# Three buffers for the pairs of transposed p, its load a step later, and later stages shifted by a step

## The chip, the cores and the metric

The kernel runs on one core of a Trainium2 chip. The metric is device time in microseconds, the median of the runs made. Five engines work side by side, each on its own queue in program order: TensorE (PE in the profile, with its weight loads as PEld), VectorE (DVE), ScalarE (ACT), GpSimd (POOL), and SyncE (SP), which here only issues DMAs. A DMA whose semaphore is not there yet holds up every later DMA in SP's queue.

## What is computed

```python
xn = _layernorm(x)
# A: attention of all 2048 rows with the last W = 512 keys, 32 heads of 128
q = (xn @ wq).reshape(B, Sq, Hq, Dh)
p = softmax(einsum("bhqd,bhkd->bhqk", q, k) * Dh ** -0.5)
s = einsum("bhqk,bhkd->bhqd", p, v).reshape(B, Sq, Hq * Dh) @ wo
# B: gated MLP with a mix over the sequence
z = gelu(xn @ w_in); z1, z2 = z[..., :Fh], layernorm(z[..., Fh:])
g = w_sp @ z2 + b_sp
out = x + s * silu((z1 * g) @ w_out)
```

x is 2048 x 512, all in float32. Every matmul is made of three in float32r: each operand is split into a rounded part h and a rest l, and h h, h l and l h are summed (`mm3`, lines 63 to 67). So nearly every operand passes through a cast on ACT (the h) and a subtraction on POOL or DVE (the l, `rest`, line 59).

## The kernel before, in words

There are three stages: a short start (layernorm and transposes of the first eight row tiles), the attention loop, and the MLP's second half. The change is in the attention loop, which fills about three quarters of the time.

The loop of line 679 runs over steps t. Attention is cut into blocks: a block is one head and 512 rows of x, four steps of 128 rows each, and `where` (line 366) says which head and rows block b has. There are 128 blocks and so 512 steps (NSTEP). The first 64 blocks use the first 1024 rows, the rest the second 1024. Two blocks, eight steps, share one head's weights. Block b has steps 4b to 4b + 3. Each step is a software pipeline: the stages that run in step t belong to different earlier or later steps, by fixed distances (line 34). In program order, step t holds:

- loads of weights for later steps (lines 680 to 684, SP)
- `shares` of step t - ML (line 500): the cast of a quarter of pL to pT_h on ACT, and the rest pT_l on POOL
- `todo`: splits of weights that have arrived (ACT, POOL), and in steps 30 to some 217 the pieces of `later_x`
- `score` of step t (line 467): three matmuls to a PSUM bank of ps_step; the negated maximum nm of a row on DVE (line 474); the Exp on ACT, to prob (line 476)
- two or three matmuls of the q products of later blocks (line 447; 42 in 16 steps), each sum to a bank of ps_acc
- `pv` of step t - PL (line 509), three matmuls with pT; after a block's fourth, `pv_out` makes oT (ACT, and two rests on DVE)
- `outp` of step t - OL (line 525), three matmuls to a bank of ps_step, and the addition to sacc on DVE (line 535)
- `turned` of block t // 4 - 1, when t % 4 is 2 (line 494)
- `turn` of step t - 1 (line 478)
- the rests of `late`, on DVE; then `ends`, more DMAs

p must be transposed before `pv`. This is done in two halves. `turn` transposes 32 x 32 squares of prob on DVE into pB (line 485). A pB holds two steps, a pair; after the second one, SP stores it to DRAM as half of p_dram (line 490, in the steps t with t % 4 equal to 0 and 2). When both halves of block b are in DRAM, `turned` loads them into pL with the rows regrouped (line 498, four DMAs of 32 partitions each). So the path of p is Exp, transpose, store, load, cast and rest, `pv`. pB has two buffers (the default of pool ap, line 87), pL two, p_dram three, pT_h and pT_l four each. ps_step has four banks, from which every step takes one for its score and one for its `outp`.

`later_x` (line 265) prepares the second 1024 rows in four passes, p = 0 to 3, while the loop runs. A pass loads two row tiles a and b, normalizes and transposes them, and makes eight tiles of parts (`new_part`, line 302: b's two halves, a's two, then the sums T2, T1, T3, T4), each of which is stored to DRAM (x_dram). All these tiles come from pool xq (name rawx), five buffers of 2 KB a partition; a and b stay alive until the sums are made. A pass has 18 places, 13/5 of a step apart (line 603). At one place the stores of its list are issued ahead of its function: the stores of a's two parts stand in the same step as the cast of T2.

The last pieces of w_in are also loaded into xq in the loop's last steps, each eight steps before its split (line 564). The q products are evicted through tiles qs (line 453, three buffers). `ln_stats` (line 169) makes the mean and 1/sqrt(var + eps) of a pair of tiles; rs_t holds var + eps between the two POOL operations (line 72), and `row_stats` of `later_x` makes nb, minus mean times r.

Of the kernel before, what the change touches and what calls it, by code (L numbers as in the profile page):

```python
# [8 lines left out]
F32 = mybir.dt.float32  # L9
# [8 lines left out]
P = 128  # L18
# [10 lines left out]
NBLK = H * NQ  # L29
NSTEP = NBLK * 4  # L30
SCALE = DH ** -0.5


XL, QL, ML, PL, OL = 11, 7, 10, 12, 17
T8 = NT // 2
LEAD = 13
Q = 32
# [3 lines left out]
def mixer_kernel(ctx: ExitStack, tc: tile.TileContext, x, wh, w_in, w_sp, b_sp, w_out, out):  # L41
# [30 lines left out]
    def rsqrt(var, y, n, v):  # L72

        nc.gpsimd.tensor_scalar(v[:, :n], var, EPS, None, op0=OP.add)
        nc.gpsimd.tensor_tensor(y[:, :n], v[:, :n], power[:, :n], op=OP.pow)

    stats = ctx.enter_context(tc.tile_pool(name="stats", bufs=2))
# [7 lines left out]
    att = ExitStack()  # L85
# [1 line left out]
    ap = att.enter_context(tc.tile_pool(name="ap", bufs=2))  # L87
    wq = att.enter_context(tc.tile_pool(name="wq", bufs=2))
    zs = att.enter_context(tc.tile_pool(name="zs", bufs=2))
    xq = att.enter_context(tc.tile_pool(name="xq", bufs=5))  # L90
    sacc = sp.tile([P, T8, D], F32, name="sacc")


# [52 lines left out]


    GROUPS = [(a, a + 1) for a in range(4)] + [(a, a + 2) for a in range(4, T8, 2)]
    mv, rx = {}, {}
    X = {0: {}, 1: {}}  # L150

    def block():
# [16 lines left out]
    def ln_stats(tiles, key):  # L169
        mv[key] = stats.tile([P, 2, 2], F32, name="mv", bufs=5)  # L170
        for k, t in enumerate(tiles):
            stt = stats.tile([P, 6], F32, name="stt", bufs=4)
            nc.vector.bn_stats(stt, t)
            nc.vector.bn_aggr(mv[key][:, k, :], stt)
        n = len(tiles)
        r = stats.tile([P, 2], F32, name="rs_r", bufs=5)
        rsqrt(mv[key][:, :n, 1], r, n, stats.tile([P, 2], F32, name="rs_t", bufs=4))
        for k in range(n):
            rx[key + k] = mv[key][:, k, 0:1], r[:, k:k + 1]

# [84 lines left out]
    def later_x(p):  # L265

        a, b = T8 + p, T8 + 4 + p
        t, nb = {}, {}

        def load():  # L270
            for i in (a, b):
                t[i] = xq.tile([P, 512], F32, name="rawx")
                nc.sync.dma_start(t[i], x[i * P:(i + 1) * P, :])

        def row_stats():
            ln_stats([t[a], t[b]], 100 * (p + 1))
            for k, i in enumerate((a, b)):
                mean, r = rx[100 * (p + 1) + k]
                nb[i] = stats.tile([P, 1], F32, name="nb", bufs=2)
                nc.gpsimd.tensor_scalar(nb[i], mean, r, -1.0, op0=OP.mult, op1=OP.mult)  # L280

        def apply(i):
            nc.scalar.activation(t[i], t[i], AF.Identity, bias=nb[i], scale=rx[100 * (p + 1) + (i == b)][1])

        def parts(i, n):
            ps = flip(t[i]).rearrange("p c q -> p (c q)")
            if n:
                nc.scalar.copy(t[i][:, :256], ps[:, :256])
            for h in range(2):
                sl = ps[:, 256 * h:256 * h + 256]  # L290
                hi, lo = new_part((h, n))
                nc.scalar.copy(hi, sl)
                late.append((rest, nc.vector, lo, sl, hi))
            if n:
                late.append((rest_f32, t[i][:, 256:], ps[:, 256:], t[i][:, :256]))
            else:
                late.append((row_sums, ps, t[b], t[a]))

        def rest_f32(to, x0, x1):
            nc.vector.tensor_tensor(to, x0, x1, op=OP.subtract)  # L300

        def new_part(k):
            st = t[k] = xq.tile([P, 512], F32R, name="rawx")
            return st[:, :256], st[:, 256:]

        def sum_part(k, src):
            hi, lo = new_part(k)
            nc.scalar.copy(hi, src())
            rest(nc.gpsimd, lo, src(), hi)

        def store(*ks):
            for k in ks:
                nc.sync.dma_start(xd[1, k][:, :, :, p * P:(p + 1) * P],
                                  t[k].bitcast(F32).rearrange("p (a c q) -> p a c q", a=2, q=P))

        def half(i, h):
            return lambda: t[i][:, 256 * h:256 * h + 256]

        seq = [load, None, None, None, None, row_stats, None,
               lambda: apply(b),  # L320
               lambda: parts(b, 1),
               lambda: apply(a),
               None,
               lambda: parts(a, 0),
               None,
               lambda: sum_part("T2", half(a, 1)),
               lambda: sum_part("T1", half(a, 0)),
               lambda: sum_part("T3", half(b, 1)),
               lambda: sum_part("T4", half(b, 0))]
        stores = {10: ((0, 1), (1, 1)), 13: ((0, 0), (1, 0)), 14: ("T2",), 15: ("T1",), 16: ("T3",), 17: ("T4",)}  # L330
        return [(f, stores.get(n, ())) for n, f in enumerate(seq + [None])], store
# [31 lines left out]
    pB = [None]  # L363
# [86 lines left out]
    def q_evict(g, k):  # L450
        ps = qps[g, BANK[k]]
        if k in (0, 2, 3):
            t = qps[g, "t", k] = ap.tile([P, 512], F32, name="qs", bufs=3)
            nc.scalar.activation(t, ps, AF.Copy, scale=SCALE)  # L454
        elif k in (1, 5):
            nc.vector.scalar_tensor_tensor(ps, ps, SCALE, qps[g, "t", {1: 0, 5: 2}[k]], op0=OP.mult, op1=OP.add)
        elif k == 4:
            t = qps[g, "t", 3]
            nc.vector.scalar_tensor_tensor(t, ps, SCALE, t, op0=OP.mult, op1=OP.add)
# [18 lines left out]
    def turn(t):  # L478

        b, j = divmod(t, 4)
        if j % 2 == 0:
            pB[0] = ap.tile([P, 4, 2, P], F32, name="pB")
        nc.vector.transpose(pB[0][:, :, j % 2, :].rearrange("p a (c q) -> p a c q", q=Q),  # L485
                            prob.pop(t).rearrange("p (a c q) -> p a c q", a=4, q=Q))
        if j == 0:
            pD[b] = dram.tile([2, P, 1024], F32, name="p_dram", bufs=3)
        if j % 2:
            nc.sync.dma_start(pD[b][j // 2], pB[0].rearrange("p a j f -> p (a j f)"))  # L490
        if j == 3:
            nc.vector.reciprocal(sums[b], sums[b])

    def turned(b):
        pL[b] = ap.tile([P, 8, 256], F32, name="pL")
        of = pD.pop(b).rearrange("s (i r) (a f) -> a r (s i) f", i=4, a=4)
        for a in range(4):
            nc.sync.dma_start(pL[b][Q * a:Q * a + Q], of[a])
# [50 lines left out]
    def plan(key, k, t, lead=6):  # L549
        loads.setdefault(max(T0, t - lead), []).append((key, k))  # L550
        at(t, lambda: split_piece(key, k, nc.vector if t >= NSTEP - 4 and k % 2 else nc.gpsimd))
# [9 lines left out]
    for n, ds in enumerate(((-16, -14, -12, -10), (-6, -4, -2, 2), (1, 4, 8, None), (13, None, 9, 11))):  # L561
        for k, d in enumerate(ds):
            if d is not None:
                plan(("w", n), k, NSTEP + d, 8)

    for key, k, d in ((("w", 2), 3, 7), (("w", 3), 1, 10)):
        loads.setdefault(NSTEP + d, []).append((key, k))
# [111 lines left out]
    for t in range(T0, T1):  # L679
        for key in loads.get(t, ()):  # L680
            if isinstance(key, int):
                load_q(key)
            else:
                load_piece(*key)
        bq, cq = divmod(t + QL, 4)
        bm, cm = divmod(t - ML, 4)
        bp, cp = divmod(t - PL, 4)
        bo, jo = divmod(t - OL, 4)
        i = t + XL
        if i < T8:  # L690
            ln_flip(i)
        if 0 <= bm < NBLK:
            shares(bm, cm)
        for f, args in todo.get(t, ()):
            f(*args)
        if 0 <= t < NSTEP:
            score(t)
        if i + 2 < T8:
            ln_apply(rows[i + 2], i + 2)
        if t in FILL:  # L700
            z1_piece(*FILL[t])
        if 0 <= bq < 4:
            qproj(bq, cq)
        g, s = divmod(t + LEAD, 16)
        if 0 < g < NG:
            q_products(g, s)
        if 0 <= bp < NBLK:
            pv(bp, cp)
        if 0 <= bo < NBLK:
            outp(bo, jo)  # L710
        if t in DRAIN:
            ps = z1_product(*DRAIN[t])
        if 0 <= bq < 4:
            qproj_out(bq, cq)
        for f, *args in q_events.get(t, ()):
            f(*args)
        if 0 <= bp < NBLK:
            pv_out(bp, cp)
        if t in DRAIN:
            z1_out(*DRAIN[t], ps)  # L720
        if t % 4 == 2 and 0 <= t // 4 - 1 < NBLK:
            turned(t // 4 - 1)
        if 0 <= t - 1 < NSTEP:
            turn(t - 1)
        while late:
            f, *args = late.pop(0)
            f(*args)
        for f, *args in ends.get(t, ()):
            f(*args)
# [279 lines left out]
```

## Time and profile before

| | us |
|---|---|
| median of 3 runs | 1965.47 |
| lowest and highest | 1961.61 and 1967.25 |
| the profiled execution | 1965.79 |
| its span, first to last instruction | 1964.0 |
| DVE idle ahead of line 485, until a store of p_dram had landed | 228.4 |
| PE idle ahead of the score's first matmul, until DVE's sacc | 81.2 |

The span is one execution; what lies around it is 1.8 us. "Busy" counts the time in which an engine has an instruction under way. In the lines of groups, the numbers after the bar are the busy time in us, the mean ns of one, then the idle time of the engine just before them and what ended it. In the windows the columns are the start and end, the length, the busy us of each engine with its instructions, the granted clock as a share, the mean share of time that the 16 DMA engines are busy, and GB/s. The lines themselves stand in the prediction.

### The profile page before, as it was taken

Reading aid. Unit: us, or ns where it says so; the run is one execution under the profiler, and the core shown is the slowest. Engines: PE = TensorE matmul, PEld = TensorE weight load, DVE = VectorE, ACT = ScalarE, POOL = GpSimd, SP = SyncE. Lnnn points to the kernel's source line nnn. Section 1 sums busy time; section 2 is a strip of 40 time slices with the busy share of each in tenths; the row PEclk is TensorE's granted clock in tenths of the full one; section 3 lists DMA queues with packets and bytes.
Section 4 is the critical chain, followed back from the end, with each engine's and each line's share of the span. In section 5 each row is a group of like instructions: output and inputs, shape, how many; then the busy total and the mean of one; then the engine's idle time right before and its main releaser. Section 6 shows DMA issues by size and latency. Waiting matters only on the chain.

```text
span 1964.0 us, 28248 instructions
## 1 busy us (share of the span) xinstructions
PE 1851.8 (94%) x8658; PEld 1551.2 (79%) x8658; DVE 1394.3 (71%) x2497; ACT 1187.8 (60%) x2631; POOL 1250.5 (64%) x1185
## 2 busy tenths in 40 slices
PE   8998999999999998899999999999999999999999
PEld 7776777777777776777777777777777899999998
DVE  5577888878888877778788778878887656333433
ACT  4666666767767666666667666666676535333422
POOL 3677788778888877777878778877887435000000
PEclk9999999999999999999999999999999999999999
DMA  5698898988998989898888988888889843544432
GB/s 174 197 267 215 229 268 232 245 246 236 252 252 236 252 236 327 227 256 232 243 216 225 242 227 229 238 226 223 226 241 252 240 145 115 188 145 160 155 128 93
DMA packets 277624, 429.16 MB, mean 219 GB/s; under 512 B 22272, under 2 KB 183808, under 8 KB 276320
## 3 DMA queue, kind: packets, MB, share of 16 engines
q1 hardware_dynamic: 272864, 421.72, 76.9%
q10 hardware_dynamic: 4608, 5.64, 0.8%
q8 instruction: 68, 1.11, 0.2%
q14 instruction: 84, 0.69, 0.1%
HBM read 260.55 MB, written 166.72 MB: 218 GB/s over the span
## 4 chain that ended last, share of the span: by engine, by line
DMA 37%; PE 34%; DVE 16%; ACT 6%; issue 4%; SPq 2%; POOL 1%; ACTq 0%; DVEq 0%; POOLq 0%
DMA p_dram<-pB 32%; DVE nm L474 5%; PE ps_g L67 4%; PE ps_g L66 4%; PE ps_g L65 4%; DVE pB L485 4%; DVE sacc L535 3%; DMA pL<-p_dram 3%; PE ps L65 3%; PE ps_a L65 3%; PE ps_a L66 3%; PE ps_a L447 3%; PE ps_a L67 2%; PE ps L67 2%; PE ps L66 2%
## 5 line engine op out<-in xcount | busy, mean ns | idle before, releaser
L59 POOL TENSOR_TENSOR pT_l<-pL,pT_h 128x512 fp32r<-128x512 f32 x507 | 655.5, 1293 | 313.0 <-ACT pT_h L505 284.9
L476 ACT ACTIVATE prob<-ps,nm 128x512 f32<-128x512 f32 x512 | 352.8, 689 | 384.3 <-DVE nm L474 381.1
L485 DVE STREAM_TRANSPOSE pB<-prob 128x512 f32<-128x512 f32 x512 | 359.1, 701 | 253.6 <-DMA p_dram<-pB 228.4
L447 PE MATMUL ps_a<-x,x 128*128 128x512 f32 x1302 | 381.4, 394 | 0.8 <-ACT qs L454 0.8
L535 DVE SCALAR_TENSOR_TENSOR sacc<-ps,sums,sacc 128x512 f32<-128x512 f32 x496 | 364.8, 736 | 20.6 <-PE ps L67 20.1
L505 ACT CAST pT_h<-pL 128x512 fp32r<-128x512 f32 x512 | 317.4, 620 | 97.8 <-DMA pL<-p_dram 70.2
L474 DVE TENSOR_REDUCE nm<-ps 128x1 f32<-128x512 f32 x512 | 340.0, 664 | 7.0 <-PE ps L67 6.9
L65 PE MATMUL ps<-wh,qT_h 128*128 128x512 f32 x512 | 213.6, 417 | 86.8 <-DVE sacc L535 81.2
L447 PEld LDWEIGHTS ps_a<-x,x 128*128 128x128 f32 x1302 | 246.6, 190 | 56.0 <-ACT qs L454 1.2
L59 POOL TENSOR_TENSOR wl<-raw,wh 128x512 fp32r<-128x512 f32 x192 | 248.7, 1296 | 9.1 <-ACT wh L141 9.1
L65 PEld LDWEIGHTS ps<-wh,qT_h 128*128 128x128 f32 x512 | 97.2, 190 | 147.8 <-DVE sacc L535 94.7
L65 PE MATMUL ps<-wh,oT_h 128*128 128x512 f32 x512 | 201.7, 394 | 5.8 <-DVE sacc L535 4.4
L66 PE MATMUL ps_a<-pT_l,wh 128*128 128x512 f32 x512 | 202.2, 395 | 4.2 <-POOL pT_l L59 4.2
L65 PE MATMUL ps_a<-pT_h,wh 128*128 128x512 f32 x512 | 202.2, 395 | 0.6 <-ACT pT_h L505 0.6
L67 PE MATMUL ps<-wh,qT_l 128*128 128x512 f32 x512 | 202.0, 395 | 0.0
L66 PE MATMUL ps<-wl,qT_h 128*128 128x512 f32 x512 | 201.9, 394 | 0.0
L67 PE MATMUL ps_a<-pT_h,wl 128*128 128x512 f32 x512 | 200.9, 392 | 0.0
L66 PE MATMUL ps<-wl,oT_h 128*128 128x512 f32 x512 | 200.7, 392 | 0.0
L67 PE MATMUL ps<-wh,oT_l 128*128 128x512 f32 x512 | 200.4, 391 | 0.0
L66 PE MATMUL ps_g<-z_l,x 128*128 128x344 f32 x512 | 164.2, 321 | 1.1 <-POOL z_l L59 1.1
L65 PE MATMUL ps_g<-z_h,x 128*128 128x344 f32 x512 | 164.4, 321 | 0.0
L67 PE MATMUL ps_g<-z_h,x 128*128 128x344 f32 x512 | 164.4, 321 | 0.0
(203 smaller groups left out, 3239.1 us busy)
## 6 DMA issues: line engine op xcount, KB each, us to landing
p_dram<-pB SPq DMA_DIRECT2D x256, 512.0 KB, 6.8
pL<-p_dram SPq DMA_DIRECT2D x512, 256.0 KB, 5.6
raw<-wh SPq DMA_DIRECT2D x194, 256.0 KB, 7.0
wq<-wh SPq DMA_DIRECT2D x62, 256.0 KB, 8.2
x<-w_sp SPq DMA_DIRECT2D x60, 256.0 KB, 5.7
x_dram<-rawx SPq DMA_DIRECT2D x32, 256.0 KB, 6.9
x<-x_dram SPq DMA_DIRECT2D x28, 256.0 KB, 6.8
u_dram<-uB SPq DMA_DIRECT2D x15, 384.0 KB, 2.3
```

The source lines that it names most:

```text
L59: engine.tensor_tensor(lo, whole, hi.bitcast(F32), op=OP.subtract)
L65: nc.tensor.matmul(ps, lh, rh, start=first, stop=False)
L66: nc.tensor.matmul(ps, lh, rl, start=False, stop=False)
L67: nc.tensor.matmul(ps, ll, rh, start=False, stop=last)
L447: nc.tensor.matmul(qps[g, bank], wt["q", g, k][a][:, c * P:(c + 1) * P], X[g * 2 // H][ORDER[k]][:, b, c], start=first, stop=r == 5, skip_ ...
L474: nc.vector.tensor_reduce(nm, ps, axis=AX.X, op=OP.max, negate=True)
L476: nc.scalar.activation(prob[t], ps, AF.Exp, bias=nm, accum_out=sums[b][:, j:j + 1])
L485: nc.vector.transpose(pB[0][:, :, j % 2, :].rearrange("p a (c q) -> p a c q", q=Q), prob.pop(t).rearrange("p (a c q) -> p a c q", a=4, q=Q))
L505: nc.scalar.copy(h, p)
L535: nc.vector.scalar_tensor_tensor(at, ps, rs, at, op0=OP.mult, op1=OP.add)
```

## The change

pB gets three buffers of its own. `turned` runs in the steps with t % 4 equal to 3 instead of 2, and behind `turn` instead of ahead of it. The distances ML, PL and OL of the three stages behind it grow by one, so the loop is one pass longer. To make room, xq has four buffers instead of five and qs two instead of three; nb, a tile of its own until now, is written into rs_t, and the w pieces are loaded six steps ahead of their split instead of eight.

```diff
--- before.py
+++ after.py
@@ -31,7 +31,7 @@
 SCALE = DH ** -0.5
 
 
-XL, QL, ML, PL, OL = 11, 7, 10, 12, 17
+XL, QL, ML, PL, OL = 11, 7, 11, 13, 18
 T8 = NT // 2
 LEAD = 13
 Q = 32
@@ -87,7 +87,7 @@
     ap = att.enter_context(tc.tile_pool(name="ap", bufs=2))
     wq = att.enter_context(tc.tile_pool(name="wq", bufs=2))
     zs = att.enter_context(tc.tile_pool(name="zs", bufs=2))
-    xq = att.enter_context(tc.tile_pool(name="xq", bufs=5))
+    xq = att.enter_context(tc.tile_pool(name="xq", bufs=4))
     sacc = sp.tile([P, T8, D], F32, name="sacc")
 
 
@@ -146,7 +146,7 @@
 
 
     GROUPS = [(a, a + 1) for a in range(4)] + [(a, a + 2) for a in range(4, T8, 2)]
-    mv, rx = {}, {}
+    mv, rx, tmp = {}, {}, {}
     X = {0: {}, 1: {}}
 
     def block():
@@ -174,7 +174,8 @@
             nc.vector.bn_aggr(mv[key][:, k, :], stt)
         n = len(tiles)
         r = stats.tile([P, 2], F32, name="rs_r", bufs=5)
-        rsqrt(mv[key][:, :n, 1], r, n, stats.tile([P, 2], F32, name="rs_t", bufs=4))
+        tmp[key] = stats.tile([P, 2], F32, name="rs_t", bufs=4)
+        rsqrt(mv[key][:, :n, 1], r, n, tmp[key])
         for k in range(n):
             rx[key + k] = mv[key][:, k, 0:1], r[:, k:k + 1]
 
@@ -276,7 +277,7 @@
             ln_stats([t[a], t[b]], 100 * (p + 1))
             for k, i in enumerate((a, b)):
                 mean, r = rx[100 * (p + 1) + k]
-                nb[i] = stats.tile([P, 1], F32, name="nb", bufs=2)
+                nb[i] = tmp[100 * (p + 1)][:, k:k + 1]
                 nc.gpsimd.tensor_scalar(nb[i], mean, r, -1.0, op0=OP.mult, op1=OP.mult)
 
         def apply(i):
@@ -450,7 +451,7 @@
     def q_evict(g, k):
         ps = qps[g, BANK[k]]
         if k in (0, 2, 3):
-            t = qps[g, "t", k] = ap.tile([P, 512], F32, name="qs", bufs=3)
+            t = qps[g, "t", k] = ap.tile([P, 512], F32, name="qs", bufs=2)
             nc.scalar.activation(t, ps, AF.Copy, scale=SCALE)
         elif k in (1, 5):
             nc.vector.scalar_tensor_tensor(ps, ps, SCALE, qps[g, "t", {1: 0, 5: 2}[k]], op0=OP.mult, op1=OP.add)
@@ -481,7 +482,7 @@
 
         b, j = divmod(t, 4)
         if j % 2 == 0:
-            pB[0] = ap.tile([P, 4, 2, P], F32, name="pB")
+            pB[0] = ap.tile([P, 4, 2, P], F32, name="pB", bufs=3)
         nc.vector.transpose(pB[0][:, :, j % 2, :].rearrange("p a (c q) -> p a c q", q=Q),
                             prob.pop(t).rearrange("p (a c q) -> p a c q", a=4, q=Q))
         if j == 0:
@@ -561,7 +562,7 @@
     for n, ds in enumerate(((-16, -14, -12, -10), (-6, -4, -2, 2), (1, 4, 8, None), (13, None, 9, 11))):
         for k, d in enumerate(ds):
             if d is not None:
-                plan(("w", n), k, NSTEP + d, 8)
+                plan(("w", n), k, NSTEP + d, 6)
 
     for key, k, d in ((("w", 2), 3, 7), (("w", 3), 1, 10)):
         loads.setdefault(NSTEP + d, []).append((key, k))
@@ -718,10 +719,10 @@
             pv_out(bp, cp)
         if t in DRAIN:
             z1_out(*DRAIN[t], ps)
-        if t % 4 == 2 and 0 <= t // 4 - 1 < NBLK:
-            turned(t // 4 - 1)
         if 0 <= t - 1 < NSTEP:
             turn(t - 1)
+        if t % 4 == 3 and 0 <= t // 4 - 1 < NBLK:
+            turned(t // 4 - 1)
         while late:
             f, *args = late.pop(0)
             f(*args)
```

## The prediction

> **What bounds the kernel now.** I read the page first: its busy shares, its chain, the costliest groups and the DMA issues.
>
> ```profile
> span 1964.0 us, 28248 instructions
> ...
> PE 1851.8 (94%) x8658; PEld 1551.2 (79%) x8658; DVE 1394.3 (71%) x2497; ACT 1187.8 (60%) x2631; POOL 1250.5 (64%) x1185
> ...
> DMA p_dram<-pB 32%; DVE nm L474 5%; PE ps_g L67 4%; PE ps_g L66 4%; PE ps_g L65 4%; DVE pB L485 4%; DVE sacc L535 3%; DMA pL<-p_dram 3%; PE ps L65 3%; PE ps_a L65 3%; PE ps_a L66 3%; PE ps_a L447 3%; PE ps_a L67 2%; PE ps L67 2%; PE ps L66 2%
> ...
> L59 POOL TENSOR_TENSOR pT_l<-pL,pT_h 128x512 fp32r<-128x512 f32 x507 | 655.5, 1293 | 313.0 <-ACT pT_h L505 284.9
> ...
> L485 DVE STREAM_TRANSPOSE pB<-prob 128x512 f32<-128x512 f32 x512 | 359.1, 701 | 253.6 <-DMA p_dram<-pB 228.4
> ...
> L505 ACT CAST pT_h<-pL 128x512 fp32r<-128x512 f32 x512 | 317.4, 620 | 97.8 <-DMA pL<-p_dram 70.2
> L474 DVE TENSOR_REDUCE nm<-ps 128x1 f32<-128x512 f32 x512 | 340.0, 664 | 7.0 <-PE ps L67 6.9
> L65 PE MATMUL ps<-wh,qT_h 128*128 128x512 f32 x512 | 213.6, 417 | 86.8 <-DVE sacc L535 81.2
> ...
> p_dram<-pB SPq DMA_DIRECT2D x256, 512.0 KB, 6.8
> pL<-p_dram SPq DMA_DIRECT2D x512, 256.0 KB, 5.6
> ...
> x_dram<-rawx SPq DMA_DIRECT2D x32, 256.0 KB, 6.9
> ```
>
> PE is 94% busy, yet 32% of the chain is one store, the turned p going to DRAM. The transpose (L485) idled 228.4 us for a free pB, and the score matmul 81.2 us for DVE's sacc: DVE waits for the store, then PE for DVE. SyncE's own waits tell why the store is late:
>
> ```profile
> SPq L498 <- DMA p_dram<-pB: 516.5, 141, 7.9
> SPq L490 <- DVE sums L492: 302.2, 109, 5.5
> ```
>
> The load of pL (L498) sits at the head of SP's queue for 516.5 us, 3.7 us a time, until the second store of its block has landed. `turned` is called ahead of `turn`, so the first store of the next block is queued behind it. One round in the timeline, SP and DVE:
>
> ```profile
> 601.26 1.81 SPq L498 DMA_DIRECT2D pL<-p_dram  x4
> ...
> 603.16 2.36 SPq L490 DMA_DIRECT2D p_dram<-pB  x2
> ...
> 605.71 0.74 DVE L535 SCALAR_TENSOR_TENSOR sacc<-ps,sums,sacc 128x512 f32<-128x512 f32 x1
> ...
> 609.84 0.71 DVE L485 STREAM_TRANSPOSE pB<-prob 128x512 f32<-128x512 f32 x1 [3.39 <-DMA p_dram<-pB]
> ...
> 611.37 1.81 SPq L498 DMA_DIRECT2D pL<-p_dram  x4
> ```
>
> The store issued at 603.16 goes out right behind the load, late; DVE stops from 606.4 to 609.8 for its buffer; the score, two steps on, finds no free bank. Now what the loop costs a step: the windows of the reduction (one a step, 0.664 us), and those of all engines for the last stretch.
>
> ```profile
> 100.00:400.00 300.00, 66.25 (x100) 0.98 0.90 243
> 400.00:700.00 300.00, 69.00 (x104) 0.99 0.90 244
> 700.00:800.00 100.00, 19.87 (x30) 0.98 0.95 278
> 800.00:1100.00 300.00, 68.96 (x104) 0.99 0.88 235
> 1100.00:1500.00 400.00, 92.90 (x140) 0.99 0.87 233
> ```
>
> ```profile
> 1100.00:1500.00 400.00, 382.43 (x1636) 306.64 (x1636) 324.91 (x579) 275.26 (x634) 322.97 (x297) 0.99 0.87 233
> ```
>
> Dividing busy by 0.664 gives 99.8, 103.9, 29.9, 103.9 and 139.9 steps: 3.01, 2.89, 3.34, 2.89 and 2.86 us each. What PE alone needs, from a stretch of the timeline without a stall:
>
> ```profile
> 615.18 0.39 PE L65 MATMUL ps<-wh,qT_h 128*128 128x512 f32 x1
> ...
> 615.86 0.84 PE L447 MATMUL ps_a<-x,x 128*128 128x512 f32 x3
> ...
> 617.90 0.40 PE L65 MATMUL ps<-wh,qT_h 128*128 128x512 f32 x1
> ```
>
> That step holds 9 matmuls of attention and 3 of the q product: 12 in 2.72 us, 0.227 each, start to start. Sixteen steps hold 16 x 9 + 42 = 186 (line 436), so 42.2 us, **2.64 us a step**. In the five stretches 477.4 steps took 1400 us and PE needed 1260: 140 us are to be had there at most. The other engines need less: in the last stretch DVE works 324.9 / 139.9 = 2.32 us a step, POOL 2.31, ACT 1.97.
>
> A page bears on the size of this bound. The Trainium skill (Perfetto Trace Analysis, Identifying the Most-Contended Engine) calls matmul busy time a bad measure of headroom, because pipelined matmuls overlap, and points to the LDWEIGHTS share instead. By PE's 94% only 112 us could go in the whole kernel; the trace agrees with the page, a record lasting 0.39 us while starts lie 0.227 apart.
>
> **The change part by part.** Block b is four steps, 4b to 4b+3; `turn(t-1)` runs in step t.
>
> *Third pB.* A pair's buffer is needed again at the third pair after it instead of the second, six steps after instead of four. Counted from the store's issue, at the end of the pair's second turn, that is 5 steps of 2.7 = 13 us against 3 steps = 8 us; a store lands in 6.8 us. The 228.4 us of DVE waits go. No instruction is added.
>
> *Load a step later, behind the next store.* Four DMA issues and the wait ahead of them move from step 4b+6 to 4b+7, past the store of the next block's first pair in SP's queue, past the wh and wq loads of step 4b+7, and past the x_dram stores of `todo` that fall in it. In step 4b+7 `turn` handles the third quarter of a block, which issues no store, so nothing else is passed. The load cannot go earlier than it does now, since its own store lands in 6.8 us: it is issued at about the same moment, and while it waits no store of p is due until the end of step 4b+8. The SP waits of 516.5 us shrink to those that harm nobody; the store behind is no longer late. Either this or the third buffer would take most of DVE's waits alone; together they leave none.
>
> *Later stages a step later (ML, PL, OL).* The same casts, rests and matmuls, a step on. The load gets the fourth whole step between its issue and its cast; of the 70.2 us that ACT waits for pL most go, worth nothing by themselves, ACT working 1.97 us of 2.64. Weights are held a step longer: v of a head is last read in step 8h+20 and overwritten in 8h+22, wo in 8h+25 and 8h+27; the two steps left are the cover, and if they were gone ACT's cast would wait for PE. pT, oT, sums: unchanged distances or room to spare. The loop has one pass more; in it and in the first steps some work is not covered by matmuls of other stages. Bounds: nothing (PE fills the tail with z1 products) and a full step at each end, 2 x 2.9 us. I take 3.
>
> *xq, five buffers to four.* This one costs. `later_x` holds a, b and two parts; the cast of T2 (L308) stands in the same step as the store of the first two parts, and used the fifth buffer:
>
> ```profile
> 240.72 0.41 ACT L308 CAST rawx<-rawx 128x256 fp32r<-128x256 f32 x1
> ```
>
> ```profile
> 241.88 2.05 SPq L313 DMA_DIRECT2D x_dram<-rawx  x2
> ```
>
> With four it must wait for the first of these stores: 241.88 + 6.9 - 240.72 = 8.1 us in which ACT stands, with the Exp of that step and the casts of the next queued behind it, and DVE's transposes and PE's scores behind those. Four banks let PE go on for about two steps, 5.3 us. I take 3 us a pass, 12 for the four passes; bounds are 0 (all covered) and 4 x 8.1 = 32. The casts of a's parts (L292) now wait for both stores of b's parts rather than one; two or three steps lie between, and I put that into the same bounds.
>
> *qs three to two, nb inside rs_t, lead 6 for w.* Of qs never more than two are alive (t0 until k = 1, then t2 beside t3): the next write follows the last read by several steps, nothing. nb is written over the rsqrt's input after its last read, on POOL both: nothing. Six steps are 16 us for a w load, and the last ones may hold SP for a step in the drain, with only stores of s and z1 loads behind them and no p stored any more: nothing.
>
> *Sum.* What PE waits for, by the view of all waits:
>
> ```profile
> PE ps L65 <- DVE sacc L535: 86.2, 87, 6.0
> ...
> PE ps_a L66 <- POOL pT_l L59: 4.2, 6, 0.8
> ...
> PE ps L65 <- DVE sacc L533: 3.6, 2, 3.1
> ...
> PEld ps L65 <- ACT prob L476: 2.2, 3, 1.2
> ```
>
> With DVE never stopped, PE is bound by itself. I put what remains of its waits at 0.06 us a step (the three lower rows name 10 us of waits on others than sacc, 0.02 a step; I take three times that because DVE works in bursts): 2.70 us. For 99.8 + 103.9 + 103.9 + 139.9 = 447.5 steps that is 1208 us instead of 1300, -92. In 700 to 800, where x is fetched from DRAM at 278 GB/s, I give 3.0 us for 29.9 steps, -10. The loop's two ends, some 34 steps, -5. Then +3 and +12: **-92**. Bounds of the whole: 0.00 and 0.16 us of remaining waits, 27 us less or 45 more. The profiled execution took 1965.79 us, 1.8 more than its span, and the median of the runs is 1965.47, so 1965.8 - 92 = **1874 us**.
>
> **The rivals.**
>
> *DMA becomes the bound.* The rows above give 243 x 300 / 99.8 = 0.73 MB a step in the first stretch and 0.67 in the last. What the 16 engines carry when full:
>
> ```profile
> 750.00:775.00 25.00, 18.81 (x81) 14.64 (x80) 19.14 (x34) 15.49 (x36) 19.11 (x18) 1.00 1.03 315
> ...
> 825.00:850.00 25.00, 25.00 (x112) 20.71 (x111) 20.58 (x38) 18.20 (x44) 20.80 (x20) 1.00 1.01 265
> ```
>
> At 265 GB/s a step of the first half needs 2.76 us, over PE's 2.64, and one of the second 2.51, under it. Then the 204 steps of 100 to 700 settle at 2.76 + 0.06, 0.12 more than I forecast: 24 us, **1898 us**. For it speaks the share of 1.01; against it 315 GB/s in the other row, at the same share. The Trainium skill (DMA: Bandwidth & Descriptors, Specifications) gives about 358 GB/s for a core's HBM traffic; by that no stretch would be bound by DMA and the forecast would stand. The row of 265 at a full share speaks for less, so the rival keeps its chance.
>
> *DVE stays the bound.* The change does not do what it says if DVE's stops only change their cause (a wait for ACT's Exp, itself behind a pL cast or T2's). DVE's 2.32 us a step speak against it. Half of PE's 86.2 us would go, 43, less 15 for the added costs: **1938 us**.
>
> *The store and load chain takes over, slower.* From the turn to the second matmul of `pv` lie 8 steps. The chain has the wait of the turn for its place on DVE (about 1.5 us, estimated from sacc and transpose of one step), 6.8 for the store, 1.8 for the four issues, 5.6 for the load, 0.6 and 1.3 for cast and rest: 17.6 of 21.6 us at 2.70. If faster steps lengthen the two landings together from 12.4 to over 18.2 us, 8 steps take over 8 x 2.93 = 23.4 us (2.93 is the present mean of the loop) and the kernel is slower than before. The longest landings are near that:
>
> ```profile
> DMA to landing us min/median/max: 2.6/6.8/10.3
> ...
> DMA to landing us min/median/max: 3.4/5.6/12.3
> ```
>
> (stores of pB, then loads of pL). With 19.5 on the mean a step takes 24.7 / 8 = 3.09 us, 0.16 x 512 = 82 more: **2047 us**. Against it: the chain is self-limiting, a slower step asks less of DMA.
>
> *PE's floor all through.* Nothing remains and ACT's stops are hidden: 140 + 5 - 3 = 142 less would be 1824; with the stretch at 700 to 800 as forecast, **1840 us**.
>
> **How the numbers follow.** Forecast 0.60, with its own range 1852 to 1892. DMA bound 0.20, DVE still bound 0.08, PE's floor 0.05, the chain 0.07. The range from 1842 to 1920 takes in the forecast, the DMA rival and most of the floor, and leaves out DVE and the chain. Within 0.3% of the time before, about what a measurement of this kernel can tell from no change, lies only the far side of the DVE rival: 0.02. Slower is the chain's 0.07; faster 0.91.
>
> **What would show it.** Right: the transposes' wait for p_dram is gone; PE's wait for sacc is below 25 us; the reduction's windows give 2.70 us a step; SP still waits at L498 but the stores at L490 follow their turn at once; four ACT stops of some 8 us at L308 in the first half. DMA rival: share near 1.0 from 100 to 700 and ACT waiting for pL. DVE rival: the idle before L485 names ACT. Chain: landings of 9 us and more, and PE waiting at `pv`. The forecast is wrong if 1100 to 1500, where no added cost falls, does not drop below 2.75 us a step.

## The result and the profile after

The changed kernel takes 1907.9 us, the median of 4 runs from 1901.5 to 1913.1, against 1964.6 before (now of 4 runs): a ratio of 0.971 (95% interval 0.9677 to 0.9744), 57 us less. The forecast was 1874, 92 less; the range went to 1920. The changed kernel's lines lie one higher from line 177 on, so that the transpose is L486, the store L491, the load L499, the addition to sacc L536.

The page after, with the rows that answer to those of before:

```profile
span 1905.1 us, 28198 instructions
...
PE 1820.5 (96%) x8658; PEld 1540.4 (81%) x8658; DVE 1403.3 (74%) x2497; ACT 1179.1 (62%) x2631; POOL 1244.3 (65%) x1185
...
PE 73%; DMA 11%; DVE 7%; ACT 3%; POOL 3%; issue 2%; SPq 1%; ACTq 0%; POOLq 0%; DVEq 0%
...
L506 ACT CAST pT_h<-pL 128x512 fp32r<-128x512 f32 x512 | 318.1, 621 | 130.8 <-DMA pL<-p_dram 68.3
...
L486 DVE STREAM_TRANSPOSE pB<-prob 128x512 f32<-128x512 f32 x512 | 359.0, 701 | 23.2 <-ACT prob L477 22.4
...
L65 PE MATMUL ps_a<-pT_h,wh 128*128 128x512 f32 x512 | 204.2, 399 | 46.7 <-DVE qT_l L728 42.3
L65 PE MATMUL ps<-wh,qT_h 128*128 128x512 f32 x512 | 204.0, 399 | 8.6 <-DVE sacc L536 5.1
...
p_dram<-pB SPq DMA_DIRECT2D x256, 512.0 KB, 5.2
```

The store no longer heads the chain. The transpose waits for no store, and the score's wait for sacc fell from 81.2 us to 5.1. But the first matmul of `pv` now idles 46.7 us, 42.3 of them for qT_l at L728, a rest on DVE that has nothing to do with `pv`'s data. Before, it hardly waited:

```profile
L65 PE MATMUL ps_a<-pT_h,wh 128*128 128x512 f32 x512 | 202.2, 395 | 0.6 <-ACT pT_h L505 0.6
```

SP's own waits in the changed kernel:

```profile
SPq L491 <- DVE pB L486: 530.7, 127, 14.9
...
SPq L499 <- DMA p_dram<-pB: 145.0, 64, 8.1
```

The load waits 145 us instead of 516.5, and the store waits for its transpose, not for the queue. The windows of the reduction again, one instruction a step (0.662 us here: 338.8 us for 512 in the page):

```profile
100.00:400.00 300.00, 67.60 (x103) 0.98 0.93 251
400.00:700.00 300.00, 68.11 (x103) 0.99 0.91 246
700.00:800.00 100.00, 20.50 (x31) 0.95 1.00 279
800.00:1100.00 300.00, 72.01 (x109) 0.99 0.91 245
1100.00:1500.00 400.00, 96.50 (x146) 1.00 0.91 246
```

That is 102.1, 102.9, 31.0, 108.8 and 145.8 steps: 2.94, 2.92, 3.23, 2.76 and 2.74 us a step. The forecast was 2.70 in four of them and 3.0 in the third. Not all of the gain lies in the loop. The mix of the MLP's second half, which no edited line touches, is faster too. Its first matmuls of each product, before:

```profile
L65 PE MATMUL ps_g<-z_h,x x512: 321/321/322, 1650.3 to 1950.8; 128*128 128x344 f32 x171
```

and after:

```profile
L65 PE MATMUL ps_g<-z_h,x x512: 316/316/381, 1600.6 to 1892.0; 128*128 128x344 f32 x171
```

From the first to the last it is 300.5 us before and 291.4 after, 9.1 less. The loop, from the first Exp to the last, took 1496.9 us before (50.3 to 1547.2) and 1449.3 after (48.7 to 1498.0), 47.6 less. So two questions stood: what does `pv` wait for, and why does the mix gain?

### The profile page after: what moved, and what is told of

The parts are those of the page before. It is cut to its first block, busy times and chain, and to the rows that moved or that the text cites. A ratio compares the mean times of both kernels' runs of the same rounds, so it can differ in the third digit from the quotient of the medians.

```text
span 1905.1 us, 28198 instructions
## 1 busy us (share of the span) xinstructions
PE 1820.5 (96%) x8658; PEld 1540.4 (81%) x8658; DVE 1403.3 (74%) x2497; ACT 1179.1 (62%) x2631; POOL 1244.3 (65%) x1185
## 2 busy tenths in 40 slices
DMA packets 277624, 429.16 MB, mean 225 GB/s; under 512 B 22272, under 2 KB 183808, under 8 KB 276320
## 3 DMA queue, kind: packets, MB, share of 16 engines
q1 hardware_dynamic: 272864, 421.72, 79.4%
## 4 chain that ended last, share of the span: by engine, by line
PE 73%; DMA 11%; DVE 7%; ACT 3%; POOL 3%; issue 2%; SPq 1%; ACTq 0%; POOLq 0%; DVEq 0%
PE ps_a L448 11%; PE ps L65 9%; PE ps L67 9%; PE ps L66 9%; PE ps_a L65 7%; PE ps_a L66 6%; PE ps_a L67 6%; DMA pL<-p_dram 4%; PE ps_g L66 4%; PE ps_g L67 4%; PE ps_g L65 4%; DMA p_dram<-pB 2%; DVE sacc L536 2%; DVE pB L486 1%; ACT prob L477 1%
## 5 line engine op out<-in xcount | busy, mean ns | idle before, releaser
L536 DVE SCALAR_TENSOR_TENSOR sacc<-ps,sums,sacc 128x512 f32<-128x512 f32 x496 | 369.6, 746 | 149.2 <-PE ps L67 144.2
L506 ACT CAST pT_h<-pL 128x512 fp32r<-128x512 f32 x512 | 318.1, 621 | 130.8 <-DMA pL<-p_dram 68.3
L486 DVE STREAM_TRANSPOSE pB<-prob 128x512 f32<-128x512 f32 x512 | 359.0, 701 | 23.2 <-ACT prob L477 22.4
L475 DVE TENSOR_REDUCE nm<-ps 128x1 f32<-128x512 f32 x512 | 338.8, 662 | 8.6 <-PE ps L67 8.5
L65 PE MATMUL ps_a<-pT_h,wh 128*128 128x512 f32 x512 | 204.2, 399 | 46.7 <-DVE qT_l L728 42.3
L65 PE MATMUL ps<-wh,qT_h 128*128 128x512 f32 x512 | 204.0, 399 | 8.6 <-DVE sacc L536 5.1
L65 PE MATMUL ps_g<-z_h,x 128*128 128x344 f32 x512 | 162.1, 317 | 0.0
L67 PE MATMUL ps_g<-z_h,x 128*128 128x344 f32 x512 | 161.9, 316 | 0.0
L65 PEld LDWEIGHTS ps_a<-pT_h,wh 128*128 128x128 f32 x512 | 96.7, 189 | 79.2 <-DVE qT_l L728 55.0
```

The lines of the kernel that those rows point to most:

```text
L65: nc.tensor.matmul(ps, lh, rh, start=first, stop=False)
L67: nc.tensor.matmul(ps, ll, rh, start=False, stop=last)
L475: nc.vector.tensor_reduce(nm, ps, axis=AX.X, op=OP.max, negate=True)
L506: nc.scalar.copy(h, p)
L536: nc.vector.scalar_tensor_tensor(at, ps, rs, at, op0=OP.mult, op1=OP.add)
```

## The experiments

Ten kernels were run. Loop and mix are measured as above, in the profiled execution of each; the ratio is that of the timed runs to the kernel before, with its interval. The kernel before was timed anew beside each set (medians 1970.7 for e1 to e4, 1966.8 for e5 to e8, 1970.2 for e9 and e10), so a ratio does not follow exactly from the medians of the table; where medians of two sets are subtracted below, a few us are uncertain.

| kernel | median us | ratio | loop us | mix us |
|---|---|---|---|---|
| before | 1964.6 | 1 | 1496.9 | 300.5 |
| changed | 1907.9 | 0.971 (0.968 to 0.974) | 1449.3 | 291.4 |
| e1: before, nb in rs_t | 1936.4 | 0.984 (0.982 to 0.986) | 1475.8 | 291.4 |
| e2: before, load moved and stages shifted | 1915.6 | 0.972 (0.970 to 0.974) | 1447.1 | 300.5 |
| e3: before, third pB and its price | 1954.3 | 0.993 (0.991 to 0.995) | 1491.2 | 299.8 |
| e4: changed, rest of the fourth q product a step earlier | 1870.2 | 0.950 (0.948 to 0.952) | 1409.1 | 291.4 |
| e5: before, 64 bytes added | 1930.5 | 0.981 (0.978 to 0.983) | 1468.2 | 297.1 |
| e6: e4, 32 bytes added | 1887.6 | 0.959 (0.956 to 0.963) | 1426.5 | 294.4 |
| e7: e4 with two pB, five xq | 1856.5 | 0.943 (0.941 to 0.946) | 1396.2 | 291.4 |
| e8: e4, stores ahead of T2 | 1857.6 | 0.944 (0.941 to 0.947) | 1399.4 | 291.4 |
| e9: changed, nb of its own | 1932.0 | 0.980 (0.978 to 0.983) | 1461.7 | 300.5 |
| e10: e7, 128 bytes added | 1858.1 | 0.943 (0.941 to 0.945) | 1393.8 | 297.1 |

### The wait of pv: e4

```diff
-                q_events.setdefault(t0 + done + 2, []).append((q_done, g, k))
+                q_events.setdefault(t0 + done + 1, []).append((q_done, g, k))
```

> The changed kernel, with the cast and rest of the fourth q product of a group one step earlier (two steps after its last matmul become one). Theory (PSUM bank): the wait of 1.04 us in every sixteenth step, 47 us in all, goes, and nothing takes its place: 1907.9 - 45 = 1863. Rival (the bank is not the cause, DVE's order or DMA is): pv waits in the same step for another instruction, 1895 or more.

The timeline of the changed kernel shows one such wait, here in a step with t % 16 = 5. It comes back every sixteen steps, 30 times in all; 26 of the 30 last 0.96 to 1.04 us:

```profile
1202.97 0.39 PE L65 MATMUL ps<-wh,qT_h 128*128 128x512 f32 x1
1203.17 0.75 DVE L536 SCALAR_TENSOR_TENSOR sacc<-ps,sums,sacc 128x512 f32<-128x512 f32 x1 [0.77 <-PE ps L67]
...
1203.84 0.70 DVE L486 STREAM_TRANSPOSE pB<-prob 128x512 f32<-128x512 f32 x1
...
1204.47 0.14 DVE L493 RECIPROCAL sums<-sums 128x4 f32<-128x4 f32 x1
1204.52 0.66 DVE L728 SCALAR_TENSOR_TENSOR qT_l<-ps_a,qT_h 128x512 fp32r<-128x512 f32 x1
...
1205.23 0.50 PE L65 MATMUL ps_a<-pT_h,wh 128*128 128x512 f32 x1 [0.97 <-DVE qT_l L728]
```

ps_acc has four banks. Ahead of that step one holds the old group's fourth q product until L728 has read it, one the sum of `pv` of the block before, and one the new group's first sum; the new group's second sum takes the last just ahead of `pv`. So `pv`'s new block needs the bank that L728 frees, which DVE reaches only after sacc, the transpose and the reciprocal of the step before, and PE stands for 0.97 us. With PL = 12 the block began a step earlier, and the row of before shows no such wait; the shift of `pv` by one step made the two meet. In e4 the rest is done a step earlier, and the waits of `pv` in the view of waits become:

```profile
PE ps_a L65 <- DVE qT_l L728: 9.1, 3, 5.9
```

Three instead of 30 waits, 9.1 us instead of 42.3; the loop takes 40.2 us less and the kernel 37.7 us, where 45 were expected. No other wait of PE took its place. The row of 42.3 us is not the bank's price alone: two of the 30 waits, of 7.8 and 5.9 us, fall into other stalls, and e4 still has three long ones. But it is settled that this rest's time, and so the bank, held `pv`. The windows of the reduction in e4:

```profile
100.00:400.00 300.00, 69.64 (x105) 0.98 0.95 260
400.00:700.00 300.00, 71.24 (x108) 0.99 0.93 252
700.00:800.00 100.00, 20.93 (x32) 0.93 1.01 278
800.00:1100.00 300.00, 74.21 (x112) 1.00 0.94 255
1100.00:1400.00 300.00, 75.49 (x114) 1.00 0.94 249
```

With 0.662 us a reduction that is 2.85, 2.79, 3.16, 2.68 and 2.63 us a step: with the bank's wait gone the last two stretches are below the 2.70 that was forecast, the first three are not.

### Which part of the change gains: e2 and e3

e2 is the move of the load together with the shift of the later stages, and nothing else:

```diff
-XL, QL, ML, PL, OL = 11, 7, 10, 12, 17
+XL, QL, ML, PL, OL = 11, 7, 11, 13, 18
...
-        if t % 4 == 2 and 0 <= t // 4 - 1 < NBLK:
-            turned(t // 4 - 1)
         if 0 <= t - 1 < NSTEP:
             turn(t - 1)
+        if t % 4 == 3 and 0 <= t // 4 - 1 < NBLK:
+            turned(t // 4 - 1)
```

> The kernel before, with the load moved behind the store and ML, PL, OL one larger; two pB, five xq, three qs, nb of its own. Theory (the store queued behind the load is the cause of DVE's waits): they fall from 228 us to under 50 with two buffers, PE's wait for sacc from 86 to under 30, the wait of pv for a PSUM bank (47 us after the change) is there, and there is no ACT stop at T2; 1964.6 less some 45 is 1920. Rival (two buffers are too few wherever the load stands): DVE's waits stay over 120 us, 1945 or more.

The waits of e2:

```profile
DVE pB L485 <- DMA p_dram<-pB: 83.8, 49, 6.3
...
PE ps_a L65 <- DVE qT_l L727: 41.9, 30, 7.3
...
PE ps L65 <- DVE sacc L535: 13.0, 21, 5.3
```

and of SP's queue in e2:

```profile
SPq L498 <- DMA p_dram<-pB: 155.4, 74, 6.1
```

DVE's waits stay above the 50 expected, but PE's for sacc is down to 13.0, and the time is 1915.6, where 1920 was expected. The loop (1447.1 us) is as short as that of the whole change (1449.3), with two buffers of pB. The load holds SP's queue for 155.4 us instead of 516.5. The bank's wait is here too, so it belongs to the shift. No kernel was run with the move or the shift alone; for the move as the cause of DVE's gain speak SP's rows.

e3 is the other half:

```diff
-    xq = att.enter_context(tc.tile_pool(name="xq", bufs=5))
+    xq = att.enter_context(tc.tile_pool(name="xq", bufs=4))
...
-            t = qps[g, "t", k] = ap.tile([P, 512], F32, name="qs", bufs=3)
+            t = qps[g, "t", k] = ap.tile([P, 512], F32, name="qs", bufs=2)
...
-            pB[0] = ap.tile([P, 4, 2, P], F32, name="pB")
+            pB[0] = ap.tile([P, 4, 2, P], F32, name="pB", bufs=3)
...
-                plan(("w", n), k, NSTEP + d, 8)
+                plan(("w", n), k, NSTEP + d, 6)
```

> The kernel before, with three pB, four xq, two qs and the w lead of six; the load stays ahead of the store, stages not shifted. Theory (the shift of pv by a step made it need its PSUM bank before DVE's rest of the fourth q product of a group has freed one): no wait of pv for that rest, so PE waits for neither; ACT waits more for pL (68 us before and after; here over 100); 1964.6 less 138 of excess, plus 45 that stays, is some 1875, less than after the change. Rival (the load's move is what carries the gain): the store stays late, DVE waits over 100 us, 1935 or more.

1954.3 us: both accounts missed. DVE does not wait for stores any more and `pv` does not wait for the bank, as the theory had it; the time is the rival's (1935 or more), but not for the rival's reason. 1875 was far off, because another wait came forward:

```profile
ACT pT_h L505 <- DMA pL<-p_dram: 233.8, 94, 7.8
...
DVE pB L485 <- ACT prob L476: 78.9, 36, 7.5
PEld ps_a L66 <- POOL pT_l L59: 63.3, 83, 1.4
...
PE ps_a L66 <- POOL pT_l L59: 30.3, 69, 1.0
```

and in SP's queue:

```profile
SPq L498 <- DMA p_dram<-pB: 662.4, 141, 8.9
```

ACT now waits 233.8 us for pL, and behind it the Exp, the transposes and `pv`. The load, still ahead of the next store, holds SP's queue for 662.4 us, longer than before. DVE is free, but store, load and cast do not fit into the steps they have. e3 also pays for the fourth xq buffer: ACT stops 32.5 us at T2. The third buffer without the move and the shift hands most of the wait from DVE to ACT.

### The place of the tiles: e1, e5, e9, e6

e1 takes only nb out of the kernel before:

```diff
-        rsqrt(mv[key][:, :n, 1], r, n, stats.tile([P, 2], F32, name="rs_t", bufs=4))
+        tmp[key] = stats.tile([P, 2], F32, name="rs_t", bufs=4)
+        rsqrt(mv[key][:, :n, 1], r, n, tmp[key])
...
-                nb[i] = stats.tile([P, 1], F32, name="nb", bufs=2)
+                nb[i] = tmp[100 * (p + 1)][:, k:k + 1]
```

> The kernel before, with nb written into rs_t and nothing else of the change. In the profiles the mix of the MLP's second half (matmuls to ps_g) starts a matmul every 0.153 us after the change and every 0.160 before, 9 us over 1536 matmuls, though no line of it was edited; what differs is that the tiles of the left half lie 64 bytes lower, since nb is gone. Theory (place of the operands): this kernel's mix falls to 0.153 us a matmul and the time by 9 us, to 1955. Rival (the mix differs from run to run, or by what the loop leaves behind): 0.160 us and 1964, within 3.

The mix falls to 291.4 us, exactly the changed kernel's, and the loop by 21.1 to 1475.8; the time is 28 us less by the medians, 32 by the ratio, for a change that only drops a tile of one element a partition. The theory had the mix right and left out the loop. nb is written eight times in the whole kernel. e5 keeps nb, with its writes and waits, and moves the tiles the other way:

```diff
     zp.tile([P, 88], F32, name="gap")
+    stats.tile([P, 16], F32, name="pad", bufs=1)
```

> The kernel before with an unused tile of 64 bytes a partition added to the pool that holds nb; nothing is removed, nothing else edited. Removing nb alone moved the tiles of the left half down by 64 bytes and gave 0.984 of the time; this moves them up by 64, so to the other side of the place before, again a multiple of 128 away from where they lie without nb. Theory (the place matters, at odd multiples of 64 bytes the operands of the mix and the rows of the DMAs are slower): the mix starts a matmul every 0.153 us instead of 0.160, 9 us less, and the loop gains some 20 as without nb; ratio 0.984. Rival (nb's own writes or waits cost the time): ratio 1.00, mix at 0.160.

The ratio is 0.981, so it is the place and not nb. But only the loop behaves as expected (28.7 us less); the mix gains 3.4 us, not 9. DVE's wait for stores falls only from 228.4 to 201.1 us, and what changes is DMA. The queue's share of the span in the page, before:

```profile
q1 hardware_dynamic: 272864, 421.72, 76.9%
```

in e5:

```profile
q1 hardware_dynamic: 272864, 421.72, 75.8%
```

and in e9:

```profile
q1 hardware_dynamic: 272864, 421.72, 81.1%
```

Share x 16 engines x span / packets gives the engines' time a packet: 0.769 x 16 x 1964.0 / 272864 is 88.6 ns before, 86.9 in e1 (76.7% of 1931.5), 85.8 in e5 (span 1930.6), 91.8 in e9 (span 1930.2) and 88.7 in the changed kernel (79.4% of 1905.1). At the pace of the changed kernel, 64 bytes cost 3.1 ns of a packet; at the slower pace of the kernel before, 1.7 (e1) or 2.8 (e5). The figure depends on the pace as well as on the place: e2, with the tiles where they were before, has 91.8. In the kept traces the difference lies in the packets of 1024 bytes, by their number nearly all rows of the pL loads (512 loads of 256 KB are 131072 rows, of 131328 such packets): their median is 80 ns before, 74 in e1, 68 in e5, 84 in e9 and 76 in the changed kernel. The medians for 512, 2048 and 4096 bytes are the same in all five (27, 84 and 159 ns). e9 undoes e1's edit in the changed kernel:

```diff
-        tmp[key] = stats.tile([P, 2], F32, name="rs_t", bufs=4)
-        rsqrt(mv[key][:, :n, 1], r, n, tmp[key])
+        rsqrt(mv[key][:, :n, 1], r, n, stats.tile([P, 2], F32, name="rs_t", bufs=4))
...
-                nb[i] = tmp[100 * (p + 1)][:, k:k + 1]
+                nb[i] = stats.tile([P, 1], F32, name="nb", bufs=2)
```

> The changed kernel with nb as a tile of its own again, so that the tiles of the left half lie 64 bytes higher, as before the change. Theory (place; in the changed kernel the loop is not held by landings any more, so slower DMA rows cost it little): the mix goes back to 0.160 us a matmul, 9 us, and the loop loses under 8; 1907.9 + 9 to 17, some 1920. Rival (the loop still pays for slow rows as the kernel before does, 20 us): 1937.

1932.0 us, 24 more than the changed kernel by the medians and 18 by the ratios; in the profiled executions it is 9.1 in the mix and 12.4 in the loop. Some of it goes with the granted clock, which was 0.985 in this profiled execution and 0.991 in that of the changed kernel; e9's run at 0.991 took 1924.5 us, 17.5 more than that one. The loop still pays for slow packets, by the profiles more than the theory's 8, so that half of the theory fell. e6 puts 32 bytes into e4:

```diff
     zp.tile([P, 88], F32, name="gap")
+    stats.tile([P, 8], F32, name="pad", bufs=1)
```

> The changed kernel with the rest of the fourth q product a step earlier (1870 us), and an unused tile of 32 bytes a partition, so that all tiles of the left half lie 32 bytes higher. Theory (place): a shift off a multiple of 64 is no better than one off 128; the mix goes back to 0.160 us a matmul or more, 9 us and up, and the time to 1879 or over. Rival (only the offset of 64 is bad): 1870, mix at 0.153.

17 us more than e4, nearly all in the loop (17.4); the mix loses 3.0 us, not the 9 that were expected. The engines' time a packet is 91.9 ns against 89.0 in e4 (83.0% of 1887.4 and 81.2% of 1868.3), so an offset of 32 is no better for DMA than one of 64.

### What the third buffer is worth, and what it was paid with: e7, e8, e10

e7 is e4 with pB, xq, qs and the w lead as before:

```diff
-    xq = att.enter_context(tc.tile_pool(name="xq", bufs=4))
+    xq = att.enter_context(tc.tile_pool(name="xq", bufs=5))
...
-            t = qps[g, "t", k] = ap.tile([P, 512], F32, name="qs", bufs=2)
+            t = qps[g, "t", k] = ap.tile([P, 512], F32, name="qs", bufs=3)
...
-            pB[0] = ap.tile([P, 4, 2, P], F32, name="pB", bufs=3)
+            pB[0] = ap.tile([P, 4, 2, P], F32, name="pB")
...
-                plan(("w", n), k, NSTEP + d, 6)
+                plan(("w", n), k, NSTEP + d, 8)
```

e8 keeps the three pB and four xq, and has the pass of `later_x` store a's parts one place ahead of T2:

```diff
-        seq = [load, None, None, None, None, row_stats, None,
+        seq = [load, None, None, None, row_stats, None,
...
                lambda: parts(a, 0),
                None,
+               None,
...
-        stores = {10: ((0, 1), (1, 1)), 13: ((0, 0), (1, 0)), 14: ("T2",), 15: ("T1",), 16: ("T3",), 17: ("T4",)}
+        stores = {9: ((0, 1), (1, 1)), 12: ((0, 0), (1, 0)), 14: ("T2",), 15: ("T1",), 16: ("T3",), 17: ("T4",)}
```

> The changed kernel with the rest of the fourth q product a step earlier, and with two pB, five xq, three qs and the w lead of eight again. Theory (with the load moved, the third buffer is not needed, and what it was paid with costs): DVE waits some 80 us for stores, PE under 15 for sacc; the ACT stops at T2, 24 us, go, and the steps around 60 and 206 lose their 14 us; 1870 - 10 = 1860. Rival (at the faster pace two buffers are too few): DVE's waits over 150 us, PE's for sacc over 40, 1890 or more.

> The changed kernel with the rest of the fourth q product a step earlier, and the pass of later_x up to the parts of a one place earlier, so that the stores of a's parts stand one place (2.6 steps) ahead of T2's cast instead of in the same step; three pB, four xq. Theory (the four ACT stops at T2 are the price of the fourth xq buffer): ACT's 24 us of waits for x_dram fall under 6 and 12 us of the loop go, 1858. Rival (the stops are hidden): 1870, within 3.

The stop at T2 in the changed kernel's timeline (ACT stands 4.57 us for the store of a's parts):

```profile
236.44 0.41 ACT L309 CAST rawx<-rawx 128x256 fp32r<-128x256 f32 x1 [4.57 <-DMA x_dram<-rawx]
```

In e8 the waits of ACT's L309 fall from 24.3 us (e4) to 4.0 and the kernel gains 12.6 us (the loop 9.7), as expected: the price of the fourth xq buffer, shown. e7 waits for stores, yet is as fast, as its theory had it:

```profile
DVE pB L486 <- DMA p_dram<-pB: 82.6, 44, 5.2
...
PE ps L65 <- DVE sacc L536: 11.0, 18, 4.1
```

82.6 us of DVE's waits cost PE 11.0. With the load moved and the stages shifted, the third pB buys nothing that can be told (1857.6 in e8 with it and 1856.5 in e7 without, inside each other's intervals; the two differ in xq, qs and the w lead too). In the change as it is, it cost, by what was taken away for it: e9, the change without the gain of nb, is 16 us slower than e2, which has two pB. e10 asks whether landings still count in e7, with 128 bytes added:

```diff
     zp.tile([P, 88], F32, name="gap")
+    stats.tile([P, 32], F32, name="pad", bufs=1)
```

> The fastest kernel so far (1856.5 us: the load moved, stages shifted, nb in rs_t, the rest of the fourth q product a step earlier, two pB, five xq), with an unused tile of 128 bytes a partition, so that the left half lies where the kernel before plus 64 bytes had it. Theory (the loop is at PE's pace and landings no longer count, the mix depends on the place): the mix is at 0.157 us, 5.7 us more; the loop gains under 4 in the stretches full of DMA; 1856.5 + 2 to 6. Rival (landings still count): the loop gains 8 or more, 1854 or less.

The mix is 5.7 us longer, exactly as in e5, which has the tiles in the same place; the loop is 2.4 shorter, the time 1.6 more and within the intervals. The test is a small one: a packet takes 87.8 ns instead of 88.7. The same step of 128 bytes in the kernel before, from e1 to e5, took 7.6 us off the loop, so faster landings count for less here. That slower ones would not hurt is not shown; e4, in e6, paid 17.4 us for them. e7 is the fastest kernel, 0.943 of before. Its loop, in windows of the reduction:

```profile
100.00:400.00 300.00, 70.14 (x106) 0.98 0.96 264
...
1100.00:1400.00 300.00, 75.43 (x115) 1.00 0.94 249
```

With 0.662 us a reduction that is 113.9 steps in the second window, 2.63 us each, PE's own pace; and 106.0 in the first, 2.83 us, with the engines of DMA at a share of 0.96 and 264 GB/s.

## Why the prediction was right, and where it was wrong

- **What bounds the kernel, right.** The store behind the load made DVE wait, and DVE made PE wait. In e2, the move with the shift and with two pB, DVE's waits for stores fall from 228.4 to 83.8 us and PE's for sacc from 86.2 to 13.0.
- **The bound by PE, right.** 2.64 us a step was the floor; e4 and e7 reach 2.63 in 1100 to 1400. The changed kernel itself stayed above the 2.70 forecast everywhere (2.74 to 2.94 outside 700 to 800), and its 2.74 in 1100 to 1500 passes the prediction's own sign of 2.75 by a hair.
- **Third pB and moved load, half right.** "Either this or the third buffer would take most of DVE's waits alone" holds for DVE's waits (83.8 us left with one, none with the other), not for the time: 54 us for the move with the shift (0.0276 of 1964.6), 14 for the third buffer with what it was paid with.
- **Later stages, the step that failed.** "pT, oT, sums: unchanged distances or room to spare" left out the banks of ps_acc, and put the cost of the shift at 3 us for the loop's ends alone. One distance did change: `pv` moved against the q products. It cost 42.3 us by the row of waits, and 37.7 us of time in e4. The sentence that most of ACT's 70.2 us of waits for pL would go failed as well (68.3 after), and did no harm.
- **nb at nothing, wrong.** Dropping it was worth some 18 to 24 us (e9), by the place of every tile behind it. So the loss at the bank was partly made up by a gain that was not forecast: without it the change would have given 33 us by e9's median, 39 by its ratio, against the 92, and every run of e9 (1924.5 to 1939.7) lies beyond the range's upper end of 1920. That the result lies inside the range is luck.
- **The gap, added up.** In the loop the forecast's terms are -92, -10, -5 and +12, so 95 us less; measured are 47.6. e4 gives back 40.2, and nb's place had brought 12.4 that were not in the sum, so some 20 us are missing beside the bank. e4's windows put them into 100 to 800 (2.85, 2.79 and 3.16 us a step, where 2.70, 2.70 and 3.0 were forecast; T2's stops, the +12, fall into them too). The share of DMA is 0.93 to 1.01 there, but 0.94 in 1100 to 1400 as well, where the loop runs at PE's pace: that DMA is what holds the earlier stretches is not shown by any run.
- **xq at 12 us, right in size, by two errors that cancel.** e8 measures 12.6. The stops came to 22.5 us over four passes, 5.6 each on the mean and only the longest 8.1; but in e8 20.3 us less of stops (24.3 to 4.0) brought 12.6, so by that estimate some 2 us of a stop were covered, not 5.3.
- **The rivals.** DMA as the bound: in the changed kernel the share is 0.93 at 251 GB/s from 100 to 400, and the bank's wait came first. In e7 the rival is near (0.96, 264 GB/s, 2.83 us a step against 2.82 by that rival's sum). The chain of store and load did not take over: one of its signs, PE waiting at `pv`, did appear, but for the bank, and the landings (medians 5.2 and 5.8 us) are far from its 9; e3 shows what the chain does without the move and the shift. DVE stayed no bound: the idle before the transpose names ACT, as that rival had it, but with 22.4 us only. The rival of PE's floor comes to 1835 by its own terms, not 1840 (11 us, not 16, are lost to 700 to 800); nothing hangs on it.

What stays open: by what mechanism 32 or 64 bytes change DMA's packets and the mix; why 64 bytes up and 64 down, 128 apart, give a mix of 297.1 and 291.4 us; and what holds the loop in 100 to 800 once the bank's wait is gone.

## What to carry to other kernels

When a stage of a software pipeline is shifted, list every ring that it shares with stages that are not, PSUM banks first, and see who frees the bank that it will get. A buffer that removes a wait is worth only what the wait costs on the engine that bounds the kernel: in e7, 83 us of DVE's waits go with 11 of PE's. A stall that comes back every period with the same length, as here every sixteen steps with 0.97 us, points to an order of allocation rather than to traffic. And a change that adds or drops a tile moves every tile behind it: what the place is worth must be measured apart before a gain is put down to the change.

## What the runs showed of the hardware

Moving all tiles of the left half up by 64 bytes a partition, with nothing else changed, took 28.7 us off the loop and 3.4 off the mix (e5). Moving them down by 64, by dropping a tile, took off 21.1 and 9.1 (e1). The matmuls of 344 columns, 1536 in all, start every 300.5 / 1533 = 0.196 us on the mean in the one place and 291.4 / 1533 = 0.190 in the other, other work included; a record lasts 321 and 316 ns. The engines' time per DMA packet was 91.8 ns in e9 and 88.7 in the changed kernel, at equal traffic; for the packets of 1024 bytes the medians are 84 and 76 ns. And a share of 0.96 carried 264 GB/s in the loop of e7, against 315 at 1.03 in the stretch of the kernel before that fetches x. So a full share does not stand for one figure of GB/s. Two thirds of the packets are under 2 KB (183808 of 277624 by the page); that it is their number rather than the bytes that fills the engines is argued, not shown.
